# One order table for another: 934 operations of a gated-recurrence and gMLP kernel, emitted in a new order

## The chip, the cores and the metric

The kernel runs on one core of a Trainium2 chip. The metric is the device time in microseconds (us) of one launch; lower is better. Five engines work side by side, each on its own list of instructions in order: TensorE (PE, with its weight loads as PEld), VectorE (DVE), ScalarE (ACT), GpSimd (POOL) and SyncE (SP, which here issues nearly all DMA transfers). An instruction waits until the instructions of other engines whose results it needs are done, and everything behind it on its own engine waits with it.

## What is computed

Two stages: a gated linear recurrence over 768 steps for 4 batches of 8 heads of width 48, and a gMLP block on its output.

```python
B, H, S, D = q.shape                                   # 4, 8, 768, 48
for t in range(S):
    state = alpha[:, :, t, :, None] * state + np.einsum('bhd,bhe->bhde', k[:, :, t], v[:, :, t])
    y[:, :, t] = np.einsum('bhd,bhde->bhe', q[:, :, t], state)
x = y.transpose(0, 2, 1, 3).reshape(B, S, H * D)       # 4, 768, 384
h = np.maximum(x @ w_in, 0.0)                          # w_in 384 x 1024
u, v = h[..., :512], h[..., 512:]
v_n = (v - mean(v)) / np.sqrt(var(v) + 1e-06)          # over the last axis
v_s = np.einsum('ts,bsd->btd', w_spatial, v_n) + b_spatial[None, :, None]
return (u * v_s) @ w_out                               # w_out 512 x 384
```

## The kernel before

**Tiling.** The 4 x 768 rows are 24 chunks of 128 rows, six to a batch, with the eight heads side by side in 384 columns. Inside a chunk the recurrence is done as matrix products: running sums of ln(alpha) give decay factors, k is divided and q multiplied by them, both are transposed, and a masked product of scores with v is added to the product of q with the carried state. Chunks 0 and 1 are worked as a pair (`pair`), chunks 2 to 5 and 6 to 9 as two groups of four ("quads", `four_chunks`), and the other fourteen one by one (`single`, two at a time in `two_singles`).

**One chunk, in order.** SP loads alpha, k, q and v (`ac`, `kc`, `qc`, `vc`; L463 for the pair, L683 for quads, L887 for singles). ACT takes the logarithm `la`. PE sums it with triangular matrices (L488, L720, L902); ACT exponentiates into `binv` and back into the bank. `kt` is kc times binv and `qt` is qc times the bank (both through `mul`, L191, on POOL or DVE). PE transposes them (L545, L773, L990), and ACT or DVE copies the results into `kq` (L180 is ACT's copy, L182 that of the others). PE multiplies v by kt for the state update (L570, L797, L933); DVE's `zs` (L415) and the `state` and `sbd` of L191 and L182 carry the state on. Score matmuls (L588, L839, L945) are masked into `ptm` by DVE (L597, L847, L951) and summed with v in PSUM (L612, L817, L962), and ACT casts the result into `xT`.

**The gMLP.** L1007 is the one line of its matmuls. For each chunk, xT times the second half of w_in gives v, which a ReLU empties into `v_sb` (L186 on ACT, L188 on DVE); DVE takes its statistics (L1069, L1070), ACT the root (`rstd`, L1080), DVE normalizes to `vn` (L1100). xT times the first half of w_in gives u, which a ReLU empties into `uT`. Per batch, `w_spT` times vn gives the spatial mix, to which DVE adds the bias into `vs` (L1156); `gT` is vs times uT (L191, POOL or DVE); gT times w_out is copied to `o_sb` or a free `raw_w` buffer and stored by SP (L1188).

**Weights.** `fetch` (L1049) loads w_in in two halves, w_spatial in three pieces and w_out, in that order, into two `raw_w` buffers taken in turn; casts to bf16 on POOL, ACT or DVE follow, and a raw buffer is free once its casts are done. The w_spatial pieces are transposed on PE and copied into `w_spT`.

**Masks.** `quad_triangles` (L342), `quad_mask` (L345, L347) and `one_chunk` (L355, L356) build constant triangular masks for the quads and the single chunks.

**What sets the order.** The builders above only record operations with their dependencies. `replay` then walks the string `PLAN`, one word for each of the 934 operations, and emits them in its order:

```python
word, *banks = word.split("@")
op, eng = ops[int(word[1:])], LETTERS[word[0]]
for x in junk:
    cols, kind, n = re.fullmatch("([0-9]+)([#~=])([0-9]+)", x).groups()
    warm(int(cols), int(n), kind)
for slot, n in zip(op.take, banks):
    held[n] = slot
    slot.bank = n
op.emit(eng)
```

A word's letter is the engine (P, D, A, G, S for PE, DVE, ACT, POOL and SP), the number the operation, the numbers behind "@" the PSUM banks (of eight) that it takes, and ":512#0" a filler matmul ahead of it: `warm` (L244 to L247) multiplies the constant fp32 tile `junk` into 512 columns of bank 0, and nothing reads the result. Each engine runs what is its own in the order of the table, SP its loads and stores too.

Of the kernel before, what the change touches and what calls it, by code (L numbers as in the profile page):

```python
# [39 lines left out]


PLAN = """
G11 S56 D1 D4 D0 D3 D2 A60 S57 S58 S59 G7 G5 G6 P62@0:512#0:512#0:288#0 P61@1 P54@2 D55 A66 D72 A64 S105 G69
P75@2:512#3:512#3 A67 D73 A65 D70 P77@1 D78 P63@0 P52@3 A71 A74 P79@4,5 A76 A68 D80 G8 D82 P85@1,0 P88@2,6 D89 A109
P123@4 P119@7 P111@5 G9 A110 P112 P120 A113 A121 A114 P124 A125 D87 D86 S106 A122 A127 P115@1 P116 G81 G128 D90 G83
A117 A126 A118 D134 P91@6,0 S107 D135 P93 D138 G131 G137 P140@7:512#2:152#2 P146@4 S108 A53 A92 A94 A147 S12 P144@6
D132 D129 P142@5 A143 S16 D133 D139 G130 G136 P148@0,1,3:96#2 S269 D141 D149 D150 D152 P157@7,4 A145 P159@6,0:496#2
D160 A158 A164 A151 A84 S390 P165@5,2 P178@7,1 D166 D161 D167 G13 G15 G14 S20 P98@4 P95@6 G153 G154 D155 G19 A17 A99
P170@5,0 P162@4 P168@2 A18 S23 A96 A163 D100 D180 D97 G273 D179 A177 A171 A276 G274 G156 P172@3,6 D173 D174 P192@4
P188@0 A193 S392 S270 P190@1 A169 A191 G275 P183@5 A184 D185 P186@4 P194@7 S271 G21 A101 A195 D196 S389 P181@5 P175@6  # L50
G22 S26 D187 D102 P34@7,3 A182 P204@5 D35 D103 A176 A277 D36 A197 S377 D198 D104 D199 P37@6,1 A39 P201@2 P215@7 A205
S272 A202 G24 P40@3,1 D42 G25 P43@5,4 G10 A41 A44 A189 P278@2 P213@1 P287@5 A38 A288 A279 D203 D200 D206 A207 D45 D216
D208 D210 D209 A280 D292 D214 P281@3 P284@0 A285 A282 A283 G300 A290 D295 A289 D301 A286 P231@6 P227@4 P223@7 A28 P232
S484 S379 S391 P224 D225 P219@2 P305@3 P220 A306 D233 D298 D221 G399 G297 P228 P211@7 D229 P307@6 S378 G294 G27
P49@0,5 P46@1,2 S496 G291 G230 A50 P309@4 G296 A48 P303@3 S29 A308 D47 D51 P243@2 D310 D304 P244 S380 S550 D245
P331@3,6 D332 A212 S538 P325@7,4 D326 A302 G293 G299 P311@2,5,0,1 D333 D312 A381 P239@3 A393 G234 P394@7 A395 P240
G226 D241 G246 S601 D314 A396 D398 S487 S613 P382@6 P247@2 P248 D249 A385 S497 A383 P217@5 A384 P323@7,3 P235@2 P236
S486 S540 A218 A313 A330 A324 G222 D327 G315 D317 D387 P338@4,5 D339 P336@3,0 D340 P328@7 P334@6 A500 A337 G386 G397
G33 A343 P400@4,3 D402 P344@5,0 D345 A335 A329 D346 A488 S708 D316 P352@6 P349@3 G32 G318 G31 A30 P257@0:512#7 D320
G319 P347@1 P341@5 D237 S485 A353 A401 P406@2,4 A350 D351 G250 D354 P411@3,6 D413 D408 A342 P359@5 P362@7 A348 G321  # L60
A322 G495 G388 G242 A360 D407 P368@6 P251@5 P403@2 D404 D412 A542 A363 P366@7 A369 A258 A355 D356 D357 P543@6 A544
A545 P370@0 P501@2 A504 D371 D548 P254@3 A554 A252 G405 P414@4 G238 A415 P409@0 A410 P555@5 S498 A546 P489@4 A490 D372
S551 S604 A502 A491 A503 P419@1 P416@6 A420 S499 S552 S539 S541 G505 G493 G507 D367 D255 D361 S615 S553 A556 A417 A373
D374 P266@3 P260@7 P263@1 A261 P426@0 D494 D421 D506 A427 A264 A267 A557 A492 D418 S762 S614 S602 D376 D375 A422 D358
P430@6 P432@7 P508@0,2 A509 D510 D423 P428@3 A558 A612 A605 D425 D424 P434@4 P511@2 D512 S603 A513 A617 A712 P442@1
P443 P435 D433 P438@2 P439 P519@7 D429 A431 D444 D560 G547 G559 D520 G521 G522 G445 P446@1 P447 P364@7 A365 A561 D440
D436 D448 P523@2,6 P514@4,5 P562@3,0 D524 D515 P606@7 P618@2 P458@1 P459 A607 D564 D563 D460 D525 D516 P454@0 P455
A549 A608 P565@3 A609 A619 A620 G441 G449 G437 P462@1 P463 P472@6 P466@5 G610 P517@4 D622 D566 A766 A473 A518 P526@6
P578@3,2 G621 D464 D611 P624@4,7 G567 A527 G568 G465 P569@6,1 S616 A623 S720 A724 A625 D467 D580 D456 D571 P574@5
P531@2 D575 G576 S774 A778 A626 A532 P450@0 P713@4 P627@5 P451 D570 D579 D452 P528@1 A529 P635@3,7 P630@2,6 P581@0  # L70
A582 G577 D628 G461 P572@5 A573 S723 S722 P725@1 A726 S710 A727 P594@0 A595 P583@5 A584 D632 D631 D636 P633@3 D637
G629 P638@0 A634 S825 P588@5 S711 S709 A639 P640@3 A728 D596 S837 A714 A641 A715 D530 D533 P643@0 S776 D585 A644 A534
P654@7 A655 D535 D730 D645 P779@3 A597 D598 A780 A781 P590@2 A591 A589 G457 G453 P475@0 P481@1 S775 S253 S721 D642
D537 A646 P478@7 S826 A482 D599 D479 A600 P586@6 P652@2 A653 A716 S839 D647 D476 P592@5 P767@7 P656@1 S764 S763 A593
D536 D648 D649 P670@0 P671 P666@2 A829 A768 D657 D718 S765 S827 P658@4 A770 D784 S840 D587 G717 G719 G729 D672 A769
D772 P732@1,5 P667 P469@0 A470 A734 A782 G783 G771 P659 P735@7 P662@6 P663 P830@0 D733 D660 D668 A833 P747@5,2 D664
# [12 lines left out]


# [1178 lines left out]
```

## Time and profile before

| | us |
|---|---|
| median of three timed runs | 141.97 |
| the three runs | 142.15, 141.97, 141.34 |
| the profiled execution, as timed | 141.13 |
| its span in the trace | 139.4 |
| mean granted clock of TensorE, share of full | 0.996 |

The profiled execution is timed with what lies around its span, so the two rows differ by 1.73 us. In the profile a busy time is that of the matmuls and operations alone, not of issuing. A row of the timeline has the start, the busy time of a run of equal instructions, engine, line, operation, what it writes and reads, the shapes and the count; in brackets follow the idle time of that engine just before and what ended it. A row of a group has the busy total and the mean of one in ns, then the idle time ahead.

```profile
PEclk9999999999999999999999999999999999999998
HBM read 23.60 MB, written 4.72 MB: 203 GB/s over the span
```

The first row is the granted TensorE clock in 40 equal slices of the span, in tenths (9 is 90% or more); the second is what the transfers moved.

### The profile page before, as it was taken

To read this page: it belongs to the slowest core of one execution; us is meant where nothing else is said; L and a number is where in the kernel's file an instruction comes from. 1 tells how busy PE (TensorE), PEld (TensorE's weight loads), DVE (VectorE), ACT (ScalarE), POOL (GpSimd) and SP (SyncE) were. 2 spreads that over 40 slices of the span, in tenths; PEclk is the share of its full clock that TensorE was granted. 3 is DMA by queue.
4 is the path that set the end of the run, shared out by engine and by line. 5 is a ranking of instruction groups with operands and counts; after the bars stand their busy time and mean duration, and the time that the engine had idled before them with its cause. 6 is when DMAs were issued, how large, how long until landed. Compare 5 with 4: busy or idle time off the path is not lost.

```text
span 139.4 us, 5117 instructions
## 1 busy us (share of the span) xinstructions
PE 132.0 (95%) x2042; PEld 82.2 (59%) x2054; DVE 118.1 (85%) x268; ACT 105.1 (75%) x244; POOL 88.1 (63%) x150
## 2 busy tenths in 40 slices
PE   6999998999999999999999999999999999999990
PEld 3456674655576565665557665665676665565560
DVE  6378878999999989798999999899899989666750
ACT  3577988999986797989957598999497966961140
POOL 6484977992879897346519968742088975006840
PEclk9999999999999999999999999999999999999998
DMA  4999999899998898998999989797700280074044
GB/s 108 321 362 371 387 393 279 276 337 308 342 264 167 253 211 178 199 213 157 213 191 193 218 159 206 158 196 149 205 5 0 85 315 5 0 295 163 2 171 168
DMA packets 76520, 28.65 MB, mean 206 GB/s; under 512 B 63056, under 2 KB 74960, under 8 KB 76496
## 3 DMA queue, kind: packets, MB, share of 16 engines
q1 hardware_dynamic: 76464, 28.32, 77.0%
q8 instruction: 16, 0.26, 0.8%
q14 instruction: 8, 0.07, 0.2%
q0 software_dynamic: 32, 0.00, 0.0%
HBM read 23.60 MB, written 4.72 MB: 203 GB/s over the span
## 4 chain that ended last, share of the span: by engine, by line
PE 76%; DVE 10%; ACT 4%; DMA 3%; issue 2%; SPq 1%; DVEq 0%
PE bank L1007 50%; DMA qc<-in_q_dram 3%; PE bank L945 3%; PE bank L247 2%; PE bank L962 2%; PE bank L990 2%; PE bank L438 2%; PE bank L773 2%; DVE qt L191 2%; PE bank L720 2%; DVE vs L1156 2%; PE bank L902 2%; ACT xT L180 2%; DVE vn L1100 2%; PE bank L933 1%
## 5 line engine op out<-in xcount | busy, mean ns | idle before, releaser
L1007 PE MATMUL bank<-w_spT,vn 128*128 128x384 bf16 x192 | 35.9, 326 | 0.1
L191 POOL TENSOR_TENSOR gT<-vs,uT 128x384 bf16<-128x384 f32 x29 | 26.2, 916 | 14.2 <-DVE vs L1156 13.7
L191 POOL TENSOR_TENSOR kt<-kc,binv 128x384 bf16<-128x384 f32 x22 | 20.0, 920 | 15.8 <-ACT binv L909 4.5
L1007 PEld LDWEIGHTS <-vn 128*128 128x128 bf16 x192 | 17.7, 98 | 11.9 <-DVE vn L1100 1.0
L1007 PE MATMUL bank<-xT,w_in 128*128 128x384 bf16 x96 | 19.7, 326 | 0.0
L1156 DVE TENSOR_TENSOR vs<-bank,bsp_bc 128x384 f32<-128x384 f32 x31 | 16.3, 548 | 3.2 <-PE bank L1007 3.0
L951 DVE TENSOR_TENSOR ptm<-bank,mask 128x512 bf16<-128x512 f32 x28 | 17.9, 679 | 0.9 <-PE bank L945 0.8
L1007 PE MATMUL bank<-w_out_sb,gT 128*128 128x384 bf16 (+1 forms) x100 | 18.1, 320 | 0.0
L1007 PE MATMUL bank<-w_in,xT 128*128 128x512 bf16 x60 | 16.9, 379 | 1.1 <-ACT xT L180 0.4
L186 ACT ACTIVATE uT<-bank 128x384 bf16<-128x384 f32 x22 | 10.6, 494 | 8.5 <-PE bank L1007 8.5
L1069 DVE BATCH_NORM_STATS2 stats<-v_sb 128x6 f32<-128x512 bf16 x24 | 16.2, 677 | 0.6 <-ACT v_sb L186 0.6
L186 ACT ACTIVATE v_sb<-bank 128x512 bf16<-128x512 f32 x23 | 13.6, 605 | 2.8 <-PE bank L1007 2.0
L180 ACT COPY kq<-bank 128x1024 bf16<-128x1024 bf16 x15 | 14.9, 1017 | 0.8 <-PE bank L773 0.4
L1007 PEld LDWEIGHTS <-gT 128*128 128x128 bf16 x100 | 9.6, 98 | 6.7 <-DVE ptm L847 0.4
L191 DVE TENSOR_TENSOR qt<-qc,bank 128x384 bf16<-128x384 f32 x24 | 12.5, 542 | 0.5 <-ACT bank L746 0.5
L1007 PEld LDWEIGHTS <-w_in 128*128 128x128 bf16 x96 | 8.8, 98 | 6.4
L180 ACT CAST xT<-bank 128x384 bf16<-128x384 f32 x24 | 10.6, 486 | 2.7 <-PE bank L438 2.1
L247 PE MATMUL bank<-junk 128*128 128x512 f32 (+4 forms) x20 | 10.3, 641 | 1.1 <-DVE junk L1235 1.1
L415 DVE TENSOR_TENSOR zs<-bank,state 128x384 f32<-128x384 f32 x16 | 8.8, 548 | 2.0 <-PE bank L797 0.7
L191 POOL TENSOR_TENSOR state<-zs,bc 128x384 f32<-128x384 f32 x7 | 6.2, 879 | 6.6 <-DVE zs L415 6.6
L847 DVE TENSOR_TENSOR ptm<-bank,mask 128x512 bf16<-128x512 f32 x16 | 10.1, 678 | 0.0
L1007 PEld LDWEIGHTS <-xT 128*128 128x128 bf16 x72 | 6.2, 97 | 5.6 <-ACT xT L180 0.2
(163 smaller groups left out, 263.8 us busy)
## 6 DMA issues: line engine op xcount, KB each, us to landing
kc<-in_k_dram SPq DMA_DIRECT2D x14, 192.0 KB, 4.1
vc<-in_v_dram SPq DMA_DIRECT2D x14, 192.0 KB, 4.2
ac<-in_alpha_dram SPq DMA_DIRECT2D x14, 192.0 KB, 4.1
qc<-in_q_dram SPq DMA_DIRECT2D x14, 192.0 KB, 4.1
raw_w<-in_moe_w_spatial_dram SPq DMA_DIRECT2D x3, 768.0 KB, 4.7
out_dram<-raw_w SPq DMA_DIRECT2D x11, 192.0 KB, 2.1
out_dram<-o_sb SPq DMA_DIRECT2D x9, 192.0 KB, 2.0
ac<-in_alpha_dram SPq DMA_DIRECT2D x2, 768.0 KB, 8.1
```

Source lines behind the costliest of these rows:

```text
L180: nc.scalar.copy(out=out, in_=in_)
L186: nc.scalar.activation(out=out, in_=in_, func=AF.Relu)
L191: ENG[eng].tensor_tensor(out=out, in0=in0, in1=in1, op=ALU.mult)
L247: nc.tensor.matmul(out=banks[n][:, 0:cols].rearrange("p (a b) -> p a b", a=4), lhsT=junk, rhs=junk[:, None, 0:cols // 4].to_broadcast([128 ...
L415: lambda _: nc.vector.tensor_tensor(out=zs[i % 3], in0=tp(), in1=state[(i - 1) % 3], op=ALU.add),
L438: nc.tensor.matmul(out=place(y, n) if q(hp).shape == place(y, n).shape else place(y, n).rearrange("p (a t) -> p a t", a=2), lhsT=sbd[(i - ...
L847: nc.vector.tensor_tensor(out=ptm[n2][:, ci, s], in0=banks[sl.bank].rearrange("p (hp t) -> p hp t", hp=HP), in1=mask[:, 3][:, None, :].to_ ...
L945: nc.tensor.matmul(out=pt[s][:, hp, :], lhsT=kT[rows, hp, :], rhs=qT[rows, hp, :], start=True, stop=True)
L951: nc.vector.tensor_tensor(out=ptm[n2][:, ci, s], in0=banks[sl_p[s].bank].rearrange("p (hp t) -> p hp t", hp=HP), in1=mask[:, 2][:, None, : ...
L1007: nc.tensor.matmul(out=ps, lhsT=lhsT, rhs=rhs, start=first and n == 0, stop=last and n == len(pairs) - 1)
L1069: nc.vector.bn_stats(out=stats[tt % 2], in_=v_sb[n2][:, tt, :])
L1156: nc.vector.tensor_tensor(out=vs[d], in0=banks[sl.bank][:, 0:TH], in1=bsp_bc[:, th, :], op=ALU.add)
```

## The change

Only the string `PLAN` changes. It has the same 934 operations with the same computation and data; their order, their PSUM banks, the engine of 86 of them and the filler differ. The first lines, the line with operation 257 (one block of the output projection) and the last line:

```diff
 PLAN = """
-G11 S56 D1 D4 D0 D3 D2 A60 S57 S58 S59 G7 G5 G6 P62@0:512#0:512#0:288#0 P61@1 P54@2 D55 A66 D72 A64 S105 G69
-P75@2:512#3:512#3 A67 D73 A65 D70 P77@1 D78 P63@0 P52@3 A71 A74 P79@4,5 A76 A68 D80 G8 D82 P85@1,0 P88@2,6 D89 A109
...
-G33 A343 P400@4,3 D402 P344@5,0 D345 A335 A329 D346 A488 S708 D316 P352@6 P349@3 G32 G318 G31 A30 P257@0:512#7 D320
...
-S924 P928@1 A929 S930 P925@3 D926 S927 P931@6 A932 S933
+G6 S56 D4 D2 D3 D1 D0 A60 G11 P63@0:512#0:512#0:288#0 G5 S57 S59 G7 P61@1 A64 A65 P62@2 A66 G72 D8 A68 A67 A74 S58 D69
+P75@0:512#3:512#3:176#3 P54@3 D70 D73 P77@2 D78 G10 G71 A76 P79@1,4:168#4 D80 P88@2,0 P85@5,6 D82 S105 A109 P111@7
...
+S540 G318 G319 P352@7 P349@4 A30 A32 G33 P257@5 A401 A350 A399 S380 S499 P411@3,6 P406@4,1 D320 G316 A353 A258 P347@2
...
+P925@7 D926 S924 S930 P931@0 S927 D932 S933
 """
```

Filler before, in columns by the operation behind it: 1312 ahead of the first summing matmuls, then P75 1024, P140 664, P148 96, P159 496, P257 512. After: the same 1312, then P75 1200, P79 168, P142 312, P148 168, P165 104.

Of the operations that change engine, 8 ReLUs of u go from DVE to ACT and 2 the other way; 6 copies of the output from DVE to ACT and 4 the other way; weight casts 5 from POOL to ACT and 3 the other way; kt 3 from POOL to DVE and 2 the other way; gT 2 from POOL to DVE and 1 the other way; the quad triangles go from POOL to DVE; the rest are ones and twos. DVE has 229 operations before and 230 after, ACT 231 and 233, POOL 110 and 107.

Three places show how operations move. The first is GpSimd's list in the head of the program, from the first product of k (`kt0`, chunk pair 0) on, before:

```order
L191 TENSOR_TENSOR kt0_104<-kc_99,binv0_108 128x8x48
L182 COPY le_quad_84<-le_pair_82 128x128
L342 MEMSET le_quad_84 32x32 x2
L182 COPY lt_quad_85<-lt_pair_83 128x128
L342 MEMSET lt_quad_85 32x32 x2
L345 MEMSET mask_73 128x128
L347 AFFINE_SELECT mask_73<-mask_73 32x128 x4
L182 CAST sbd0_130<-state0_127 128x384
L191 TENSOR_TENSOR kt1_105<-kc_99,binv2_110 128x8x48
```

and after:

```order
L191 TENSOR_TENSOR kt0_104<-kc_99,binv1_109 128x8x48
L355 MEMSET le_one_75 128x128
L356 AFFINE_SELECT le_one_75<-le_one_75 128x128
L355 MEMSET mask_73 128x128
L356 AFFINE_SELECT mask_73<-mask_73 128x128
L182 CAST vb0_113<-vc_101 128x8x48
L345 MEMSET mask_73 128x128
L347 AFFINE_SELECT mask_73<-mask_73 32x128 x4
L191 TENSOR_TENSOR kt1_105<-kc_99,binv2_110 128x8x48
```

The quad triangles have left GpSimd, `one_chunk` (before, 20 rows further down) now stands behind the first kt, and one of the casts of v (`vb0`) has come in behind it, ahead of the quad mask; the cast of the state has left.

The second is SyncE's list of loads behind the second piece of w_spatial, before (of the two `qc_100` of L887 the first is chunk 10's):

```order
L887 DMA vc_101<-in_v_dram 128x8x48
L683 DMA kc_99<-in_k_dram 128x8x192
L683 DMA qc_100<-in_q_dram 128x8x192
L887 DMA ac_98<-in_alpha_dram 128x8x48
L1049 DMA raw_w0_96<-in_moe_w_spatial_dram 128x2x768
L887 DMA ac_98<-in_alpha_dram 128x8x48
L683 DMA vc_101<-in_v_dram 128x8x192
L887 DMA ac_98<-in_alpha_dram 128x8x48
L887 DMA qc_100<-in_q_dram 128x8x48 x2
L887 DMA kc_99<-in_k_dram 128x8x48
L887 DMA ac_98<-in_alpha_dram 128x8x48
L1049 DMA raw_w1_97<-in_moe_w_out_dram 128x4x384
```

and after (the first `qc_100` of L887 is chunk 11's, the second chunk 10's):

```order
L887 DMA qc_100<-in_q_dram 128x8x48
L683 DMA kc_99<-in_k_dram 128x8x192
L683 DMA qc_100<-in_q_dram 128x8x192
L1049 DMA raw_w0_96<-in_moe_w_spatial_dram 128x2x768
L683 DMA vc_101<-in_v_dram 128x8x192
L887 DMA ac_98<-in_alpha_dram 128x8x48
L1049 DMA raw_w1_97<-in_moe_w_out_dram 128x4x384
L887 DMA kc_99<-in_k_dram 128x8x48
L887 DMA vc_101<-in_v_dram 128x8x48
L887 DMA qc_100<-in_q_dram 128x8x48
```

The load of w_out has moved up, ahead of chunk 10's q and k; the q of chunk 11 has moved up ahead of the quad's k and q.

The third is the end of VectorE's list, before:

```order
L1156 TENSOR_TENSOR vs2_155<-bank1_65,bsp_bc_90 128x384
L188 TENSOR_SCALAR uT0_136<-bank5_69 128x384
L1156 TENSOR_TENSOR vs1_154<-bank3_67,bsp_bc_90 128x384
L1156 TENSOR_TENSOR vs0_153<-bank0_64,bsp_bc_90 128x384
L191 TENSOR_TENSOR gT1_144<-vs1_154,uT0_136 128x384
L191 TENSOR_TENSOR gT1_144<-bank6_70,uT0_136 128x384
L182 COPY o_sb3_160<-bank1_65 128x384
L182 COPY raw_w0_96<-bank3_67 128x384
```

and after:

```order
L191 TENSOR_TENSOR gT1_144<-vs3_156,uT0_136 128x384
L191 TENSOR_TENSOR gT1_144<-bank7_71,uT0_136 128x384
L1156 TENSOR_TENSOR vs2_155<-bank0_64,bsp_bc_90 128x384
L1156 TENSOR_TENSOR vs1_154<-bank4_68,bsp_bc_90 128x384
L1156 TENSOR_TENSOR vs0_153<-bank7_71,bsp_bc_90 128x384
L191 TENSOR_TENSOR gT1_144<-vs1_154,uT0_136 128x384
L182 COPY raw_w0_96<-bank7_71 128x384
L182 COPY raw_w0_96<-bank0_64 128x192
```

Of the last gate products of VectorE two stand ahead of the last three additions of the bias and one stands behind them, where before both products stood behind all additions. Its last copy is half an output block (192 columns), where it was a whole one.

More of the change, by code (lines that the diff above doesn't have):

```diff
@@ L48 @@
[L48 to L52, printed above, removed]
@@ new lines @@
+P75@0:512#3:512#3:176#3 P54@3 D70 D73 P77@2 D78 G10 G71 A76 P79@1,4:168#4 D80 P88@2,0 P85@5,6 D82 S105 A109 P111@7
+A110 P52@1 A53 P112 D87 A113 A114 D83 P119@4 P120 G9 A121 P123@6 P115@1 P124 P116 D86 D90 D89 P91@2,0 S106 G128 D81
+P93 A125 A117 G137 G134 S107 D129 A118 S108 G130 D132 G139 G133 A126 D138 S12 A122 D135 D131 P142@1:312#5 P144@7 D145
+P146@4 A94 D147 P140@0 D141 A127 A143 A55 G15 G14 A136 P148@7,3,1:168#5 A92 A13 S16 S269 D149 G150 G151 G18
+P165@0,2:104#5 P157@4,6 A164 D167 D166 D152 G153 P95@7 P159@2,5 D161 D160 G17 G154 G273 A84 A96 A19 A158 P98@6 A99
@@ new lines @@
+A504 A503 A556 G505 G547 D375 D252 D494 S552 S615 P438@6 P364@3 D421 D418 A422 D548 S551 S601 A429 D506 D423 D424
+P442@2 D425 P432@5 A433 A557 A617 P508@7,0 D549 D365 G559 D560 P511@4 P439 D512 D440 A510 S614 P446@5 P447 P443 P434@3
+G441 A558 S762 D444 A509 S604 S603 S553 D448 G513 P435 P519@2 D520 P562@7,6 P523@5,1 D525 P514@2,4 G449 D524 A564
+P458@0 D516 D436 G445 P454@1 G521 A605 S602 S708 P565@5 P606@6 A609 A563 P455 D456 P618@4 P459 D460 A619 P462@3 P430@1
+A620 A607 A608 D566 D561 G437 A431 A612 P472@0 P574@5 P463 A473 P466@7 A467 D515 P517@1 P526@2 A518 A712 A527 G621
@@ new lines @@
+A641 G785 P586@2 P588@7 P656@6 P767@1 A782 A597 D537 D598 D600 D657 D599 A587 A768 D642 S723 G731 P654@5 A655 A781
+P469@0 A470 P732@2,4 D733 P658@5 P652@0 G771 A646 D647 D648 D649 A829 A770 P670@6 P662@2 P663 P659 S776 S764 S775 A769
+D772 P666@1 P667 G783 A589 D784 D664 D660 G665 P671 D672 D668 A653 A734 P738@5,4 P786@2,3 D740 P747@6,0 D749 P830@7
+A737 A787 A831 A833 D748 P686@1 P682@2 P650@0 P743@6 D744 A832 S827 S826 S765 S265 D835 P687 P678@4 P679 D739 S268
+S837 A841 A773 P789@7 P842@6 P683 G661 G669 G673 P690@5 A788 A843 G834 G745 D688 A844 A651 P693@1 A694 D684 P741@0
```

67 lines of the change are left out of this document (28 added, 39 removed).

## Prediction

> **What bounds the kernel now.** I read the page's busy totals first, then the windows of each engine, then the same windows for the filler matmuls alone (line 247), then the timeline of the first 25 us.
>
> ```profile
> PE 132.0 (95%) x2042; PEld 82.2 (59%) x2054; DVE 118.1 (85%) x268; ACT 105.1 (75%) x244; POOL 88.1 (63%) x150
> PE 76%; DVE 10%; ACT 4%; DMA 3%; issue 2%; SPq 1%; DVEq 0%
> ```
>
> TensorE is busy 95% of the span and holds 76% of the chain that ended last. What an order table can win is what TensorE does not spend on real work; the windows say where that lies.
>
> ```profile
> 0.00:5.33 5.33, 4.28 (x6) 1.95 (x7) 2.65 (x29) 2.12 (x2) 3.51 (x16) 1.00 0.70 181
> 5.33:25.00 19.67, 18.49 (x374) 11.93 (x377) 15.39 (x27) 16.26 (x34) 13.82 (x26) 1.00 1.07 357
> 25.00:60.00 35.00, 34.03 (x599) 21.26 (x592) 32.99 (x73) 31.05 (x75) 27.43 (x41) 1.00 0.98 250
> 60.00:110.00 50.00, 49.62 (x813) 31.82 (x816) 47.92 (x101) 41.08 (x102) 30.68 (x39) 1.00 0.76 155
> 110.00:135.75 25.75, 25.59 (x270) 15.20 (x271) 18.93 (x42) 14.32 (x34) 12.66 (x31) 1.00 0.38 138
> 135.75:139.40 3.65, 0.00 (x0) 0.00 (x0) 0.27 (x1) 0.32 (x1) 0.00 (x0) 0.83 0.48 173
> ```
>
> Columns: window, its length, busy us of PE, weight load, DVE, ACT and POOL, granted clock, DMA share, GB/s. Between 5.33 and 135.75 PE idles 1.18 + 0.97 + 0.38 + 0.16 = 2.7 us. The rest of its loss is filler:
>
> ```profile
> 5.33:25.00 19.67, 5.05 (x13) 1.96 (x12) 1.00 1.07 357
> 25.00:60.00 35.00, 1.02 (x2) 0.38 (x2) 1.00 0.98 250
> ```
>
> So 6.1 us of filler and 2.7 us of idle are the whole ceiling, 6.2 us of it in the head (5.33 to 25 us), 1.99 us in 25 to 60, and 0.54 us after that. VectorE is the second wall: it is busy 32.99 of 35 and 47.92 of 50 us.
>
> **The change, part by part.** All operations stay; order, banks, filler and the engine of 86 of the 934 operations change.
>
> *Filler.* Behind the first 1312 columns, which both tables have, it falls from 2792 to 1952 columns.
>
> ```profile
> 51.43 1.28 PE L1007 MATMUL bank<-w_in,xT 128*128 128x512 bf16 x5 [0.16 <-ACT xT L180]
> 52.55 1.02 PE L247 MATMUL bank<-junk 128*128 128x512 f32 x2
> 53.40 0.81 PE L1007 MATMUL bank<-w_out_sb,gT 128*128 128x384 bf16 x4
> ```
>
> The 512 columns at 52.55 hold up the next matmul until 53.40: 0.85 us, or 1.66 ns a column. The new table has none there. In the head 2280 columns become 1952, 0.55 us less, but those columns lie where PE waits for data, so the head is worked out from what it waits for.
>
> *Head.*
>
> ```profile
> 6.82 0.91 POOL L191 TENSOR_TENSOR kt<-kc,binv 128x384 bf16<-128x384 f32 x1 [1.75 <-ACT binv L513]
> 6.92 1.21 DVE L191 TENSOR_TENSOR kt<-kc,binv 128x384 bf16<-128x384 f32 x1
> 7.80 0.93 ACT L180 CAST vb<-vc 128x384 bf16<-128x384 f32 x2 [0.31 <-DMA vc<-in_v_dram]
> 10.14 0.52 PE L570 MATMUL bank<-vb,kt 64*128 64x96 bf16 x16
> 14.29 0.58 DVE L191 TENSOR_TENSOR kt<-kc,binv 128x384 bf16<-128x384 f32 x1
> 14.58 0.74 PE L612 MATMUL bank<-ptm,vb 64*32 64x128 bf16 x64
> 17.69 0.93 DVE L182 CAST o_sb<-vc 128x384 bf16<-128x384 f32 x2 [0.30 <-DMA vc<-in_v_dram]
> 17.73 1.27 POOL L182 CAST o_sb<-vc 128x384 bf16<-128x384 f32 x2 [0.37 <-DMA vc<-in_v_dram]
> 18.88 0.94 PE L797 MATMUL bank<-o_sb,kt 32*128 32x96 bf16 x48
> 19.58 2.05 POOL L182 CAST w_in<-raw_w 128x512 bf16<-128x512 f32 x3 [0.59 <-DMA raw_w<-in_moe_w_in_dram]
> 22.60 1.47 PE L1007 MATMUL bank<-w_in,xT 128*128 128x512 bf16 x5
> 24.00 0.43 PE L817 MATMUL bank<-o_sb,ident 32*32 32x384 bf16 x8
> 31.15 0.22 POOL L355 MEMSET le_one<- 128x128 bf16 x1
> 32.07 0.37 POOL L356 TENSOR_SCALAR_AFFINE_SELECT mask<-mask 128x128 bf16<-128x128 bf16 x1
> L182 POOL CAST vb<-vc 128x384 bf16<-128x384 f32 x9 | 4.5, 505 | 0.0
> L839 PE MATMUL bank<-kq 48*128 48x128 bf16 x64 | 2.9, 217 | 0.6 <-DVE zs L415 0.5
> ```
>
> The bracket is the idle time before and its releaser. Three steps wait for a load: 7.80, 17.7, 19.58. The first eleven loads keep their order but for vc and qc of the first pair, so these times stand.
> - First pair: the second kt goes to POOL after its binv, about 7.5 to 8.4. Then POOL does `one_chunk` (four instructions; before, 31.15 to 32.44, so 1.3 us) ahead of casting vb (0.5): 8.4 + 1.3 + 0.5 = 10.2, so the update starts at 10.25, not 10.14. Loss 0.1 us.
> - DVE takes `state` and its copy sbd of chunk 1, about 0.6 each like the kt at 14.29, among the four masks: I put the summing matmuls (14.58) 0.3 us later. The quad's transposes must wait for exponentials and products anyway, and the next stop is the 17.7 load.
> - At 17.7 three casts instead of two go to POOL, but DVE casts none beside it: at 0.5 each 1.5 us, the update at 19.2 instead of 18.88. Loss 0.3 us.
> - w_in: POOL casts two thirds (2.05 x 2/3 = 1.37) and ACT the third beside it (about as long as one of POOL's, 0.68): ready at 20.95, where before the three end at 21.63 and the first v matmuls start at 22.60, behind three score groups. The new order runs a v block (0.65, half of the row at 51.43) between score groups (at most 2.9 / 8 = 0.36, its matmuls overlapping): 20.95 + 2 x 0.65 + 2 x 0.36 = 23.0 for the set that before is done at 24.00 (the row at 24.00). Ahead by 1.0 us, and by 1.3 with groups of 0.22.
> - What is late next: the groups behind need banks that ACT empties one after another (0.47 us each, half of the row at 7.80). That is two to three times a quarter to half of such a copy, 0.6 us of new waits as an estimate; hidden, they cost nothing.
>
> Net 1.0 to 1.3 less 0.6: I take **0.6 us won**, bounds 0 and 1.3.
>
> *Middle, 25 to 110 us.* The filler's 0.85 us goes; up to 0.97 us of idle might. What holds it back is DVE. By the rows below, the switched operations give DVE: uT -6 x 0.54, output copies -2 x 0.55, value casts +1 x 0.51 net, kt and gT +1 each (0.58 to 1.21), v_sb +2 x 0.68, vn +2 x 0.46, smaller ones +1.1: about +1 us in all, nearly all of it before 25 us (`state`, sbd, two kq copies, quad triangles). So behind 25 us DVE has the same work and only 2 us of idle to close up.
>
> ```profile
> L188 DVE TENSOR_SCALAR uT<-bank 128x384 bf16<-128x384 f32 x10 | 5.3, 540 | 0.0
> L191 DVE TENSOR_TENSOR gT<-vs,uT 128x384 bf16<-128x384 f32 x2 | 1.7, 867 | 0.5 <-ACT uT L186 0.5
> L182 DVE CAST o_sb<-vc 128x384 bf16<-128x384 f32 x2 | 0.9, 510 | 0.3 <-DMA vc<-in_v_dram 0.3
> L188 DVE TENSOR_SCALAR v_sb<-bank 128x512 bf16<-128x512 f32 x1 | 0.7, 676 | 0.0
> L1100 DVE TENSOR_SCALAR vn<-v_sb,mvs,rstd 128x512 bf16<-128x512 bf16 x21 | 8.9, 461 | 0.6 <-ACT rstd L1080 0.6
> ```
>
> I take **0.7 us won**, bounds 0 and 1.8.
>
> *End.* DVE now does the last-but-one half of the gate and, behind another copy, the very last output copy, where ACT took it at once (a DVE copy of 0.55 ahead of 0.3: 0.2 us later).
>
> ```profile
> 130.73 1.84 POOL L191 TENSOR_TENSOR gT<-vs,uT 128x384 bf16<-128x384 f32 x2 [0.53 <-DVE uT L188]
> 132.07 0.92 DVE L191 TENSOR_TENSOR gT<-vs,uT 128x384 bf16<-128x384 f32 x1 [0.50 <-ACT uT L186]
> ```
>
> Such a DVE product takes 0.92 beside POOL's and 0.58 alone (14.29); at 6.92 it took 1.21 and ended 0.4 us behind POOL's. In the new table both products of the last two gates become ready with one vs: one of them ends up to 0.55 us later, with three output groups (1.95 us) to hide it. I take **0.2 us lost**, bounds 0 and 0.8. The Trainium skill's "SBUF: State Buffer", section "Who interferes with whom", says that a VectorE instruction with two SBUF inputs and a GpSimd one that reads SBUF exclude each other for a whole instruction, and that issue order decides who blocks. By that rule POOL, which gets its go-ahead last, waits out DVE here; the 1.21 us row agrees, the other way round.
>
> **Sum.** -0.6 - 0.7 + 0.2 = -1.1 us: span 138.3. The profiled execution took 141.13 for 139.4 of span, so 140.0 for it; the three timed runs lie at a median of 141.97, 0.84 above, so 141.97 - 1.1 = **140.9 us**.
>
> **Rivals.**
> 1. *No change.* DVE is the wall, the head's lead runs into it and PE idles where filler stood: 0 to -0.5, about 141.7. For it: DVE 94 to 96% busy from 25 to 110. Against it: in the head DVE reaches the end of the quad's masks about 0.7 us earlier with 1 us more work done.
> 2. *Slower: late loads.* The q load of chunk 10 moves behind the 768 KB of w_out; of the 192 KB loads as many stand ahead of it as before.
>
> ```profile
> 38.34 3.05 SPq L887 DMA_DIRECT2D qc<-in_q_dram x2
> qc<-in_q_dram SPq DMA_DIRECT2D x14, 192.0 KB, 4.1
> raw_w<-in_moe_w_out_dram SPq DMA_DIRECT2D x1, 768.0 KB, 5.5
> 48.92 0.54 DVE L191 TENSOR_TENSOR qt<-qc,bank 128x384 bf16<-128x384 f32 x1
> ```
>
> Issued at 38.34 and 4.1 us on its way, it lands at 42.4, 6.5 us before its qt. At 250 GB/s w_out costs 3.1 us of queue. On DVE the qt overtakes another qt, a vs half and a zs (0.54 each), and the head's lead is 0.6: 2.2 us earlier. Slack: 6.5 - 3.1 - 2.2 = 1.2 us, by a median landing time; chunks behind it have the same. DVE runs in order, so masks, vs and z behind a late qt stand too. From a wait of 1.1 us on, the win is gone; at 2 us, w_out at half that rate, it gives +0.9, 142.9.
> 3. *A larger win*: no new waits in the head and all filler and half the idle gone: -1.3 - 1.3 = -2.6, 139.4.
> 4. *The clock drops in the head* for want of filler. Cold, 1312 columns took 4.28 us, 3.3 ns a column against 1.66: half speed, and one stretch of 3.4 us at it costs 1.7 us: +0.6, 142.6. Against it: no new pause over 0.6 us. The Trainium skill, "TensorE: Matmul & The Clock Gate", Part 1, has the clock halve after an idle window of about 3.4 us; by that rule nothing happens here, and the 0.83 clock after PE stopped at 135.75 agrees that a drop needs a long pause.
>
> **How the numbers follow.** Forecast 0.50, no change 0.23, late loads 0.15, larger win 0.08, clock 0.04. A measurement here tells about 0.5% (0.7 us) from no change. The forecast's own spread (140.2 to 141.5) leaves 0.06 of it within that: faster 0.52, same 0.29, slower 0.19. The range reaches from just below the larger win to the late loads: 139.0 to 143.0.
>
> **What would show it.** Right: upd near 19.2 and the first v matmuls near 21 us; filler after 25 us gone with DVE's share there unchanged; PE's last matmul about 1 us earlier against its first. Wrong: a DVE wait on qc between 43 and 50 us (rival 2), PE idle of over 1.5 us in 25 to 60 (rival 1), a granted clock under 1 before 25 us (rival 4). What would upset the sum most is DVE waiting in its new order for something that ACT or POOL delivers late.

## The result and the profile after

| | before | after |
|---|---|---|
| median of 20 runs each, us | 141.66 | 140.63 |
| lowest and highest, us | 140.73 to 142.43 | 139.93 to 141.97 |
| profiled execution, as timed, us | 141.13 | 140.56 |
| its span, us | 139.4 | 138.8 |

The ratio of after to before is 0.9937, with a 95% interval of 0.9909 to 0.9965: faster by 0.5 to 1.3 us, 0.9 us in the middle. The forecast was 1.1 us. Ratios leave out executions in which TensorE's clock was disturbed; the one experiment where that hides something, without filler in the head, lists all of its own.

The page of after, its busy row and the chain that ended last:

```profile
PE 133.5 (96%) x2054; PEld 82.4 (59%) x2054; DVE 117.6 (85%) x272; ACT 105.1 (76%) x246; POOL 85.9 (62%) x142
PE 94%; DVE 2%; issue 1%; DVEq 0%
```

TensorE held 76% of that chain before and holds 94% now: the ACT, DVE and DMA links have nearly all gone out of it. That share is no measure of the win, though: the page of a kernel told of below that is as fast as the new one (w_out loaded later) has 80% for TensorE and 7% for DMA. The windows of each engine in after (columns as before the change: window, length, busy us of PE, weight load, DVE, ACT and POOL, granted clock, DMA share, GB/s):

```profile
5.33:25.00 19.67, 19.64 (x387) 12.74 (x386) 15.49 (x29) 15.31 (x34) 13.27 (x26) 1.00 1.07 363
25.00:60.00 35.00, 34.95 (x636) 21.57 (x634) 33.52 (x75) 32.20 (x80) 26.31 (x34) 1.00 1.00 249
60.00:110.00 50.00, 49.84 (x766) 31.45 (x764) 46.37 (x96) 42.50 (x102) 31.38 (x40) 1.00 0.81 173
110.00:135.00 25.00, 24.83 (x265) 14.63 (x263) 18.42 (x40) 12.93 (x32) 11.29 (x29) 1.00 0.29 105
```

TensorE's idle time from 5.33 us on has shrunk from 2.7 to 0.24 us (0.41 by these rows, but the last window runs 0.17 us past its last matmul, which ends at 134.83), and VectorE does 0.53 us more than before in 25 to 60 us and 1.55 us less in 60 to 110. But not all of the 2.7 us was idle. The matmuls of the v blocks, before and after:

```profile
L1007 PE MATMUL bank<-w_in,xT 128*128 128x512 bf16 x60 | 16.9, 379 | 1.1 <-ACT xT L180 0.4 <-issue 0.2
L1007 PE MATMUL bank<-w_in,xT 128*128 128x512 bf16 x72 | 18.9, 380 | 0.0
```

Both kernels run 72; twelve of before have no record in the trace, and the 1.1 us of "idle" at their places, 0.63 us of it in 25 to 60 us, is theirs. So about 1.6 us of real idle time has shrunk to 0.24. The filler of after, in the same windows of line 247 alone, is all in the head:

```profile
5.33:25.00 19.67, 4.91 (x15) 2.31 (x14) 1.00 1.07 363
```

A busy row cannot say where a win arises, because the ends of matmuls are modelled and records can be missing. So I count work: each group of matmuls is worth the median time from its start to the next group's start in the trace of before, and the table says how much later (+) or earlier (-) than before each kernel's trace had the same amount of it behind it. The whole is 121.4 us of matmuls without filler; "new" is the table after the change, the others are experiments told of below.

| work done, us | before at, us | new | old, no late filler | new, late filler | new head, old rest | old head, new rest | new to 60, old rest |
|---|---|---|---|---|---|---|---|
| 7 | 14.87 | +0.68 | +0.45 | +0.69 | -0.01 | +0.86 | +0.69 |
| 14 | 25.18 | -0.64 | +0.41 | -0.59 | -0.75 | +1.90 | -0.59 |
| 20 | 31.21 | -0.23 | +0.41 | -0.19 | -0.20 | +2.52 | -0.19 |
| 40 | 52.28 | -0.72 | +0.48 | -0.14 | -0.33 | +1.84 | -0.55 |
| 44 | 57.10 | -1.48 | +0.20 | -0.10 | 0.00 | +1.09 | -1.30 |
| 58 | 71.50 | -1.77 | +0.68 | -0.43 | -0.11 | +0.76 | +1.18 |
| 88 | 101.66 | -1.06 | +0.61 | +0.32 | -0.19 | +1.50 | +1.09 |
| 121.3 | 135.13 | -0.92 | +0.61 | +0.45 | -0.28 | +1.63 | +1.00 |

A column is one execution, and executions of the same order differ in the head: the first quad's v lands between 16.3 and 17.7 us, and TensorE's first matmuls take longer for a time that varies (worked out in the part on the head below). So differences down a column say more than one number. The new table's column: 0.7 us late in the first pair, which will turn out to be that longer time and not the order; 0.6 early at 25 us, of which 0.2 are left at 31; 1.5 early at 57; and from 71 us to the end 0.85 of it is given back. A part of these regional numbers is the weighting of the groups; the last row is free of that.

### The profile page after: what moved, and what is told of

Read it like the earlier page. It is cut to its first block, busy times and chain, and to the rows that moved or that the text cites. A ratio compares the mean times of both kernels' runs of the same rounds, so it can differ in the third digit from the quotient of the medians.

```text
span 138.8 us, 5131 instructions
## 1 busy us (share of the span) xinstructions
PE 133.5 (96%) x2054; PEld 82.4 (59%) x2054; DVE 117.6 (85%) x272; ACT 105.1 (76%) x246; POOL 85.9 (62%) x142
## 4 chain that ended last, share of the span: by engine, by line
PE 94%; DVE 2%; issue 1%; DVEq 0%
PE bank L1007 56%; PE bank L247 6%; PE bank L945 3%; PE bank L962 3%; PE bank L773 3%; PE bank L990 3%; PE bank L438 3%; PE bank L720 2%; PE bank L858 2%; PE bank L902 2%; PE bank L839 2%; PE bank L933 2%; PE bank L400 1%; PE bank L797 1%; PE bank L1019 1%; PE bank L817 1%
## 5 line engine op out<-in xcount | busy, mean ns | idle before, releaser
L191 POOL TENSOR_TENSOR kt<-kc,binv 128x384 bf16<-128x384 f32 x21 | 19.5, 939 | 20.4 <-ACT binv L909 6.5
L1007 PE MATMUL bank<-w_in,xT 128*128 128x512 bf16 x72 | 18.9, 380 | 0.0
L1069 DVE BATCH_NORM_STATS2 stats<-v_sb 128x6 f32<-128x512 bf16 x24 | 16.3, 680 | 0.2
L186 ACT ACTIVATE uT<-bank 128x384 bf16<-128x384 f32 x28 | 13.4, 495 | 3.6 <-PE bank L1007 3.4
L186 ACT ACTIVATE v_sb<-bank 128x512 bf16<-128x512 f32 x21 | 12.6, 603 | 3.3 <-PE bank L1007 3.2
L1007 PEld LDWEIGHTS <-gT 128*128 128x128 bf16 x100 | 9.0, 98 | 6.1 <-DVE kq L182 0.4
L1100 DVE TENSOR_SCALAR vn<-v_sb,mvs,rstd 128x512 bf16<-128x512 bf16 x23 | 9.8, 452 | 1.2 <-ACT rstd L1080 1.2
L247 PE MATMUL bank<-junk 128*128 128x512 f32 (+5 forms) x20 | 9.2, 585 | 1.1 <-DVE quarters_of L324 1.1
```

The lines of the kernel that those rows point to most:

```text
L186: nc.scalar.activation(out=out, in_=in_, func=AF.Relu)
L191: ENG[eng].tensor_tensor(out=out, in0=in0, in1=in1, op=ALU.mult)
L247: nc.tensor.matmul(out=banks[n][:, 0:cols].rearrange("p (a b) -> p a b", a=4), lhsT=junk, rhs=junk[:, None, 0:cols // 4].to_broadcast([128 ...
L1007: nc.tensor.matmul(out=ps, lhsT=lhsT, rhs=rhs, start=first and n == 0, stop=last and n == len(pairs) - 1)
L1069: nc.vector.bn_stats(out=stats[tt % 2], in_=v_sb[n2][:, tt, :])
L1100: ENG[e].tensor_scalar(out=vn[n2][:, x, :], in0=v_sb[n2][:, x, :], scalar1=mvs[n2][:, x, 0:1], scalar2=rstd[n2][:, x:x + 1], op0=ALU.subtr ...
```

## Experiments

All are edits of the two order tables; times are medians, ratios against the kernel before.

### The filler at 52.55 us, taken out of the old table and put into the new

```diff
-P257@0:512#7
+P257@0
```

> The table of before without the one filler ahead of operation 257 (512 columns at 52.55 us); nothing else differs. Theory A (TensorE sets the time, the filler stood on its path): 0.85 us faster than before, TensorE's last matmul at about 134.9 in the trace. Theory B (VectorE, busy 94 to 96% from 25 to 110 us, sets the pace, and the filler only filled a pause): within 0.2 us of before, with as much idle time on TensorE between 50 and 60 us as the filler took.

Measured: 141.68 us beside 141.70 for before, ratio 0.9985 (0.9960 to 1.0009). TensorE's rows at the place:

```profile
51.61 1.51 PE L1007 MATMUL bank<-w_in,xT 128*128 128x512 bf16 x6
53.51 0.82 PE L1007 MATMUL bank<-w_out_sb,gT 128*128 128x384 bf16 x4 [0.39 <-DVE ptm L847]
69.03 0.66 PE L1007 MATMUL bank<-w_spT,vn 128*128 128x384 bf16 x3 [0.52 <-DVE vn L1100]
```

Theory B holds, in the main. Where the filler stood, the same block of the output projection now waits 0.39 us for VectorE's mask product, which has yet to read the bank that the block takes (bank 0), and a later block waits 0.52 us for a normalization: the filler lay over waits. In the table above the column gains 0.28 us between 40 and 44 and has lost it by 58.

```diff
-P257@5
+P257@5:512#1
```

> The new table with 512 columns of filler put back ahead of operation 257. Theory A: 0.85 us slower than the new table, so level with before (0 to -0.1 us). Theory B: the new table's order has slack for it there, since TensorE then waits less for VectorE behind it: no slower than the new table, -0.9 us against before.

Measured: 141.52 us, ratio 0.9982 (0.9955 to 1.0010), 0.0045 or 0.6 us behind the new table's 0.9937. The trace of this one:

```profile
52.54 1.02 PE L247 MATMUL bank<-junk 128*128 128x512 f32 x2
53.40 0.81 PE L1007 MATMUL bank<-w_out_sb,gT 128*128 128x384 bf16 x4
54.15 0.62 PE L945 MATMUL bank<-kq 48*128 48x128 bf16 x16
```

Theory A here: in the new table the same 512 columns cost what they take, 0.86 us on TensorE, and no wait behind them gets shorter. (This execution also waited 0.50 us for ScalarE ahead of 40.40, where its order is the new table's and the new table's trace has no such wait; that part of its column is not the filler's.) So the new order has no wait at that place and the old one had. TensorE's rows around it show what stands there. Before, behind the filler at 52.55 and one block of the output projection:

```profile
54.15 0.41 PE L858 MATMUL bank<-ptm,vb 128*32 128x128 bf16 x16
...
55.04 0.62 PE L945 MATMUL bank<-kq 48*128 48x128 bf16 x16
55.69 0.33 PEld L1007 LDWEIGHTS <-xT 128*128 128x128 bf16 x3 [0.20 <-ACT xT L180]
55.92 0.60 PE L1007 MATMUL bank<-w_in,xT 128*128 128x512 bf16 x2 [0.26 <-ACT xT L180]
```

And after:

```profile
52.02 0.82 PE L1007 MATMUL bank<-w_out_sb,gT 128*128 128x384 bf16 x4
52.77 0.62 PE L945 MATMUL bank<-kq 48*128 48x128 bf16 x16
53.32 0.41 PE L858 MATMUL bank<-ptm,vb 128*32 128x128 bf16 x16
...
54.22 0.34 PE L933 MATMUL bank<-vb,kt 128*128 128x96 bf16 x4
54.40 0.81 PE L1007 MATMUL bank<-w_out_sb,gT 128*128 128x384 bf16 x4
```

L858 needs VectorE's masks. Before, it was next behind that block; after, the scores of the next two chunks (L945) stand ahead of it, and an update and a second output block follow at once. They are real work in the place of the filler. (The 0.26 us at 55.92 is no wait: weights of three matmuls are loaded at 55.69 and two matmuls are recorded. Nor is the 0.16 us at 51.43 that the prediction shows: five of six are recorded there.) The block's bank changes too, from 0 to 5; which of the two, order or bank, takes the wait away was not tried apart.

### The two tables cut at 25 us and at 61 us

The first words are one table's; all others follow in the other table's order, with its engines, banks and filler.

```diff
 words 1 to 140 of the new table: ... P170@4,5 A171 A177
-P162@6 P194@0
+P162@6 S390 S20 S23 A163 A276 ... (the table of before)
```

> The first 140 words of the new table (up to about 25 us), then all others in the order, on the engines and in the banks of before, with its filler ahead of 257. Theory A (the head's lead of 0.6 us at 25 us carries to the end, less what is paid back by 30 us): 0.3 to 0.6 us faster than before. Theory C (the whole win is the late filler and the lead is eaten by VectorE): within 0.1 us of before.

Measured: 141.41 us, ratio 0.9979 (0.9950 to 1.0007): 0.3 us faster, and 0.28 in the trace's last row, at the lower end of theory A; theory C and no change at all are not excluded by the interval. The lead of 0.75 at 25 us has shrunk to 0.2 by 31 us and to 0 by 57.

```diff
 words 1 to 140 of the table of before: ... D180 D97 G273 D179
+G10 A169 A171 A177 P194@0 ... (the new table)
```

> The first 140 words of the table of before, then all others as in the new table, so without the late filler. Theory A: 0.3 to 0.6 us faster than before (the filler's 0.85 and the pauses of 0.3 less the 0.5 to 0.8 us that the new order loses behind 60 us). Theory C: 0.9 us faster, as the new table.

Measured: 142.74 us, ratio 1.0079 (1.0043 to 1.0114), slower by 1.1 us: neither theory. It loses 1.35 us at the seam, in one wait of a v block for ScalarE:

```profile
26.46 0.87 ACT L180 CAST vb<-bank 128x384 bf16<-128x384 f32 x2
...
27.39 0.81 PE L1007 MATMUL bank<-w_in,xT 128*128 128x512 bf16 x3 [1.35 <-ACT vb L180]
```

The block takes a bank that ScalarE has yet to empty; the whole new table has no such wait there. Behind the seam the column wins 1.43 us between 31 and 57 us and gives 0.87 back behind 71, as the new table does (1.25 and 0.85). So what the new order wins and loses behind 31 us seems to be its own, and not the head's lead at work; the seam stands between this and a proof.

```diff
 words 1 to 434 of the new table: ... P419@2 A420 A367 D357
+S601 S708 P501@2 A504 D548 ... (the table of before)
```

> The first 434 words of the new table (up to about 61 us), then all others in the order, on the engines and in the banks of before. Theory D (the new order wins 1.2 us between 25 and 57 us whatever follows, and its own order behind 60 us gives some 0.5 us of it back): 1.3 to 1.5 us faster than before, 0.4 to 0.6 faster than the new table. Theory E (the order of before cannot keep the lead, because VectorE is 95% busy there and stops TensorE until the lead is gone): no better than the new table, 0.5 to 0.9 us faster than before, with new waits of TensorE for VectorE between 60 and 90 us.

Measured: 142.00 us beside 141.42, ratio 1.0045 (1.0016 to 1.0074). Theory D falls at the seam, which costs 2.5 us, and what was to be shown (the new order's give-back left out) wasn't; theory E's waits for VectorE are not the main ones either. The waits of TensorE in 60 to 75 us (releaser, us, times, longest):

```profile
PE bank L902 <- ACT v_sb L186: 0.7, 1, 0.7
PE bank L1007 <- DVE vn L1100: 0.7, 1, 0.7
PE bank L902 <- ACT raw_w L180: 0.6, 1, 0.6
```

Two of three are again banks that ScalarE empties too late for the order that follows.

### Order without its engines, and engines without their order

27 operations between words 140 and 434 of the new table run on another engine than before; these alone are exchanged. Two of them:

```diff
 ... in the new table
-D226 A31
+G226 G31
```

> The new table with the 27 operations between its words 140 and 434 (about 25 to 61 us) that changed engine put back on their engine of before; order, banks, loads and filler are the new ones. Theory I (the order of TensorE's work wins the middle: it has other matmuls to run where it waited for a mask): within 0.3 us of the new table, 0.6 to 0.9 faster than before. Theory J (the engines of these 27 win it, each step of an order holding only with them): at least 0.6 us slower than the new table, with TensorE waiting for VectorE or ScalarE between 25 and 61 us.

Measured: 145.63 us, ratio 1.0290 (1.0250 to 1.0329). The largest of five stops between 25 and 66 us:

```profile
35.82 0.85 ACT L180 COPY w_spT<-bank 128x384 bf16<-128x384 bf16 x2
...
36.34 0.32 PE L711 MATMUL bank<-la,lt_quad 128*128 128x384 bf16 x1 [1.29 <-ACT w_spT L180]
```

A copy that VectorE did at once in the new table is now behind ScalarE's other work, and the next sums need its bank. Theory J's first half holds.

```diff
 ... in the table of before
-G226 G31
+D226 A31
```

> The table of before with the same 27 operations on the engines that the new table gives them, everything else as before, with the filler ahead of 257. Theory I: no faster than before (0 to 1 us slower, since the order was not made for them). Theory J: 0.5 us or more faster than before.

Measured: 147.22 us, ratio 1.0376 (1.0328 to 1.0424). Theory J's second half falls: the new engines in the old order are the worst of all. Theory I, that the order alone wins, fell with the run before. Each is worth something only with the other. The one trace shows no single place: eleven waits of TensorE of 0.2 to 0.5 us between 25 and 66 us. That execution (149.69 us) also had the clock at half for 3.4 us in the head, which the last section comes back to.

### The load of w_out

```diff
-S29 S378 S392 ... S379 S484 ... S390 ... S538
+S378 S392 ... S379 S484 ... S390 ... S538 S29
```

(and cast A31 of w_out behind it, beside the others). It passes six loads, not the seven that the expectation counts.

> The new table with the load of w_out moved back by seven loads, behind the q, k and v of chunks 10 and 11 (and its second cast beside the other three). Theory D (the order of TensorE's and VectorE's work wins; w_out lands 6.5 us ahead of its first cast in the new trace): within 0.2 us of the new table, 0.7 to 0.9 us faster than before. Theory F (the loads worked out anew carry the middle's win, since TensorE needs w_out at 52 us): 0.4 us or more slower than the new table, with TensorE waiting for a cast of w_out at 52 us.

Measured: 140.61 us, ratio 0.9945 (0.9915 to 0.9976), the new table's own time within the interval. The load takes 6.1 us here and lands about at its first cast, yet TensorE doesn't wait for it. Theory F falls: where the load of w_out stands earns nothing.

### The head

```diff
-G10 G71 ... P79@1,4:168#4
+G71 G10 ... P79@1,4
```

> The new table with the first pair's cast of v ahead of one_chunk on GpSimd and without the 168 columns of filler ahead of the first state update. Theory A (the head waits for the quad's load of v at 17.4 us, which swallows what the first pair loses): the first update 0.4 us earlier (10.6 to 10.2), the quad's update unchanged, within 0.2 us of the new table. Theory K (the first pair's 0.4 us count): 0.4 us faster than the new table.

Measured: 140.45 us, ratio 0.9923 (0.9891 to 0.9955), 0.2 us from the new table and inside its interval. One of the first summing matmuls (L488), the first update (L570) and the quad's (L797), the new table first:

```profile
6.14 0.53 PE L488 MATMUL bank<-la,lt_pair 128*128 128x384 bf16 x1
10.59 0.51 PE L570 MATMUL bank<-vb,kt 64*128 64x96 bf16 x16
19.18 0.97 PE L797 MATMUL bank<-o_sb,kt 32*128 32x96 bf16 x48
```

and this kernel:

```profile
6.03 0.32 PE L488 MATMUL bank<-la,lt_pair 128*128 128x384 bf16 x1
9.93 0.51 PE L570 MATMUL bank<-vb,kt 64*128 64x96 bf16 x16
18.95 1.17 PE L797 MATMUL bank<-o_sb,kt 32*128 32x96 bf16 x48
```

Of the 0.66 us by which the first update is earlier, 0.35 are there at the transposes of kt already (8.53 us against 8.88), ahead of the edit: the loads of the pair land within 0.1 us of the new table's, but the same summing matmul takes 0.32 us in one execution and 0.53 in the other. That leaves 0.31 for the edit, and nothing of it is left at the end of the second update, which begins 0.23 earlier and ends 0.03 earlier. Theory A fits this trace; the times, 0.2 us apart, can't tell it from theory K.

The reason that theory A gives holds only in part. The kernel with w_out loaded later has the new table's head unchanged, and its trace has:

```profile
9.86 0.51 PE L570 MATMUL bank<-vb,kt 64*128 64x96 bf16 x16
18.89 0.81 PE L797 MATMUL bank<-o_sb,kt 32*128 32x96 bf16 x45 [0.17 <-POOL o_sb L182]
```

Its first update comes 0.73 us ahead of the new table's, and its quad's update ends 0.45 us ahead, though GpSimd starts to cast the quad's v at 17.43 us in one and 17.48 in the other. So a part of an early start gets past that load. It is gone at TensorE's last matmul, which ends at 134.78 and 134.83 us.

```diff
-G15 G14 ... A13
+G13 G15 G14
```

> The new table with all three casts of the first half of w_in on GpSimd one behind the other, as before, instead of two there and one on ScalarE. Theory A (this split starts the first v matmul early and makes the head's lead): the first v matmul at 21.7 to 21.9 us instead of 21.1, the lead at 25 us down from 0.6 to about 0, and 0.3 to 0.6 us slower than the new table. Theory L (the lead is spent by 30 us anyway): within 0.2 us of the new table.

Measured: 141.27 us, ratio 0.9986 (0.9955 to 1.0018), 0.7 us slower than the new table by the two ratios. Theory A by its time; but the place is not shown. The profiled execution was its fastest (140.74), its loads landed early, its first v matmul came at 20.59 us and not at 21.7 or later, and in its trace the lead at 25 us is 0.95 us, no smaller than in other kernels with the new head (0.73 in the one above). The cost of that cast's engine stays open.

```diff
-P75@0:512#3:512#3:176#3 ... P79@1,4:168#4 ... P142@1:312#5 ... P148@7,3,1:168#5 ... P165@0,2:104#5
+P75@0 ... P79@1,4 ... P142@1 ... P148@7,3,1 ... P165@0,2
```

> The new table without the 1952 columns of filler between 6.9 and 20.5 us (the first 1312 stay). Theory A (they fill waits for loads): within 0.2 us of the new table, first update of the state 0.3 to 0.9 us earlier but the quad's update still at 19.2 us, behind its load of v. Theory H (they keep TensorE's clock up): a granted clock under 1 or matmuls of twice the length in the head, and 0.3 us or more slower than the new table.

Measured: 142.41 us, from 140.44 to 145.29. The one execution with a mean granted clock of 0.997 took 140.44, like the new table; the other eleven had 0.970 to 0.988 and took 141.17 to 145.29. The windows of the profiled one (143.91 us):

```profile
7.00:8.50 1.50, 0.54 (x5) 0.30 (x4) 1.12 (x3) 1.50 (x6) 0.37 (x1) 1.00 1.11 368
8.50:10.40 1.90, 1.22 (x13) 0.87 (x14) 0.57 (x2) 1.23 (x2) 1.75 (x6) 0.97 1.09 372
10.40:17.10 6.70, 6.52 (x63) 3.39 (x63) 5.72 (x10) 3.46 (x7) 2.39 (x7) 0.50 1.09 380
17.10:25.00 7.90, 7.13 (x206) 5.03 (x205) 5.68 (x11) 6.50 (x15) 5.78 (x9) 1.00 0.83 267
```

The clock is at half from 10.4 to 17.1 us. Theory H holds: without the head's filler the clock drops in most executions. That the filler otherwise only fills waits, as theory A says, rests on the one execution without a drop.

### Two operations back on ScalarE

```diff
-D561 ... D932
+A561 ... A932
```

> The new table with two operations back on ScalarE, where the table of before has them: the cast of v for chunk 15 (VectorE, 75.75 us, 0.85 us long beside a GpSimd product; TensorE waits 0.31 for it) and the last output copy. Theory D: the wait at 75.75 goes, 0.3 us, and the end comes 0.15 us earlier: 0.45 us faster than the new table, 1.2 to 1.4 faster than before. Theory G (the wait is only taken over by the next one behind VectorE): 0.15 us faster than the new table.

Measured: 140.55 us beside 141.42, ratio 0.9910 (0.9874 to 0.9946): 0.4 us ahead of the new table by the ratios, whose intervals overlap. The wait that it was to remove, in the new table:

```profile
75.47 0.91 POOL L191 TENSOR_TENSOR kt<-kc,binv 128x384 bf16<-128x384 f32 x1 [0.28 <-ACT binv L909]
75.69 0.81 PE L1007 MATMUL bank<-w_out_sb,gT 128*128 128x384 bf16 x4
75.75 0.85 DVE L182 CAST vb<-vc 128x384 bf16<-128x384 f32 x1
76.65 0.33 PE L933 MATMUL bank<-vb,kt 128*128 128x96 bf16 x4
```

and without it:

```profile
75.95 0.81 PE L1007 MATMUL bank<-w_out_sb,gT 128*128 128x384 bf16 x4
76.60 0.33 PE L933 MATMUL bank<-vb,kt 128*128 128x96 bf16 x4
```

From the output block to the update it is 0.65 us instead of 0.96, so the wait is gone. Its last copy, on ScalarE again, ends 0.36 us behind the last matmul, where the new table's ends 0.53 behind. At the last matmul its trace has 0.97 us on before and the new table's 0.92. Whether 0.3 us of it stays can't be told from six executions. It and the kernel with v's cast ahead of the mask have the lowest medians measured, and neither is told apart from the new table.

## Why the prediction was right in its sum, and where it wasn't in its steps

**The sum.** 1.1 us were forecast, 0.9 measured; 140.9 us against 140.63, with the median of before itself 0.3 us lower in the longer series. Its terms were 0.6 us won in the head, 0.7 in the middle and 0.2 lost at the end. At the prediction's own borders the two traces have 0.64 us won at 25 us, 0.42 more at 101.66, and 0.17 lost between the last matmul and the last copy. Inside the middle 0.4 us is lost from 25 to 31 us, 1.25 won from 31 to 57, 0.3 more by 71, and 0.85 given back behind that. So the middle was put too high, pieces that the prediction doesn't have cancel there, and that the sum came out is in part luck.

**Filler.** The step said that the 512 columns at 52.55 hold up the next matmul and cost 0.85 us. In the old table they don't: without them the time is the same within 0.4%. The number was read from the row that follows the filler, and that row cannot show that the matmul behind it would have had to wait anyway. The amount did go, since the new order has other work ready there; put back into it, the filler costs 0.6 us.

**Head.** The quad's update was put at 19.2 us and came at 19.18; the first v matmuls at 20.95, and they came at 21.09; the lead of 0.6 at 25 us was met. That they fit so closely is luck: in the traces of seven kernels that have the new head unchanged the quad's update starts between 18.44 and 19.42 us and the first v matmul between 20.60 and 21.33.

For the first pair 0.1 us of loss was forecast, and in the two traces the update came 0.44 later, at 10.59. But those two executions are not alike. At first a matmul takes longer: the summing matmuls took 0.33 us in the trace of before, from 5.33 us on, and 0.53 in that of after, at 6.14; and where that ends differs from one execution to the next. Two in which it ended late, the old head (first words old, rest new; two rows) and the new one (new order, old engines; its L488 row at 6.14 is that of after, and the next two matmuls took 0.53 and 0.49):

```profile
6.54 0.53 PE L488 MATMUL bank<-la,lt_pair 128*128 128x384 bf16 x1
11.01 0.51 PE L570 MATMUL bank<-vb,kt 64*128 64x96 bf16 x16
10.83 0.51 PE L570 MATMUL bank<-vb,kt 64*128 64x96 bf16 x16
```

In these two the new head's first update comes 0.2 us earlier and not later; in two where the summing matmuls took 0.33 us or less from the first on, it came at 9.86 (w_out loaded later) and the old one's at 10.14 (before). So the loss of 0.1 us is not borne out, and neither is one of 0.44. The path was right: the update at 10.59 follows `one_chunk` and the cast of v on GpSimd, which ends at 10.53. The prediction had both kernels start alike, and nothing in it says how far two executions of one head lie apart. What failed is the step from 25 us to the end: a lead there was taken as won, and the new head in front of the old rest is worth 0.3 us, if anything.

**Middle.** 0.7 us with an upper bound of 1.8 was taken for 25 to 110 us. The bound counts 0.97 us of idle time in 25 to 60 us, of which 0.63 is matmuls without a record. In 31 to 57 us the new order wins 1.25 us, about the 0.85 of the filler's place and the 0.34 that really was idle. The reason given for less, that VectorE is full and only 2 us of its idle time could be closed, was the wrong measure: VectorE is no less busy there (33.52 us against 32.99), but TensorE has something else to run while it waits for it. That the new order would lose anything behind 60 us was in no step; 0.85 us of it were lost behind 71. The wait for the cast at 75.75 is 0.31 us of that; where the rest goes is not shown.

**End.** Right, and the kernel with its last copy back on ScalarE gets those 0.17 us again. The last copy ends 0.53 us after TensorE's last matmul (134.83 to 135.36), where it was 0.36 (135.75 to 136.11). Where the gate products of VectorE and GpSimd collide, GpSimd's last two take 2.11 us, where they took 1.84, with output blocks to hide it:

```profile
130.53 2.11 POOL L191 TENSOR_TENSOR gT<-vs,uT 128x384 bf16<-128x384 f32 x2 [0.29 <-DVE vs L1156]
131.30 0.56 DVE L191 TENSOR_TENSOR gT<-vs,uT 128x384 bf16<-128x384 f32 x1
134.53 0.82 DVE L182 COPY raw_w<-bank 128x384 f32<-128x384 f32 x2 [2.67 <-PE bank L1007]
```

**Rivals.** Late loads: q of chunk 10 landed 1.31 us ahead of its product where 1.2 us had been reckoned, and moving w_out later changed nothing. No change, by VectorE as the wall: its wall is real for the old order (the run without the late filler), not for the new. The clock in the head: it stayed at 1.00 from 5.33 us on in the profiled execution of the new table, but the reason given, that no new pause is long enough, was wrong; the run without the head's filler had no pause over 0.95 us and lost the clock.

## What to carry to other kernels

A filler or a pause next to a busy engine is not a win to be read off its row: take it out alone first, since what it covers may be as long. Count the records of a kind before reading a short gap as a wait: a missing record looks the same. An order, its engines and its banks are one thing; parts of a better table in another's place were 0.6 to 5.3 us slower in four of five tries here, and in three of the four the longest waits were for banks that another engine had yet to empty. A lead at one point is worth only what is left of it at the last matmul. And two traces compare in their first 20 us only if their first matmuls became fast at about the same time.

## What was not expected of the hardware

TensorE's clock fell to half without a pause of over 1.22 us. In the run without the head's filler, from 7.0 to 10.4 us TensorE was busy 1.76 of 3.4 us, its longest idle times 0.95 and 0.61 us:

```profile
8.11 0.38 PE L545 MATMUL bank<-ident,kt 128*128 128x128 bf16 x4 [0.95 <-ACT bc L520]
9.10 0.40 PE L545 MATMUL bank<-ident,kt 128*128 128x128 bf16 x4 [0.61 <-POOL kt L191]
```

and the clock was 0.50 for the 6.7 us that followed, in which it was busy 6.52. The Trainium skill, "TensorE: Matmul & The Clock Gate", Part 1, speaks of an idle window of about 3.4 us; here such a window was half busy and it fell all the same. Nor is filler a guarantee: the profiled execution of the old order with the new engines, which has the old head with all its filler, lost the clock too, after a window in which TensorE was busy 2.11 of 3.4 us (9.6 to 13.0) with a pause of 1.22 us in it; from 13.0 to 16.4 us it was granted 0.51.

Another thing: one VectorE cast of v takes 0.35 us alone at 67.88 and 0.85 at 75.75, where GpSimd's product runs from 75.47 to 76.38: it ends 0.22 us behind it. The Trainium skill, "SBUF — State Buffer", section "Who interferes with whom", says that a VectorE cast can use ports that it shares with GpSimd, and that whoever issues first then has them for its whole instruction while the other is blocked. These rows agree in the main: the cast that begins second ends only behind the product, though 0.22 us behind it and not the whole 0.35 that it takes alone:

```profile
67.88 0.35 DVE L182 CAST vb<-vc 128x384 bf16<-128x384 f32 x1
```
